# GpSimd's subtractions beside the statistics, and a written order for token groups 2 and 3, in an FNet and ReGLU kernel

## The chip, the cores and the metric

The kernel runs on one core of a Trainium2 chip. The metric is the device time of one execution in microseconds (us); lower is better. The shown time is the median of several executions.

The core's engines run side by side and wait for each other by semaphores: TensorE (PE in the profile; its weight loads are PEld), VectorE (DVE), ScalarE (ACT), GpSimd (POOL), and SyncE (SP), which issues transfers. GpSimd issues transfers too. Each engine works through its own instructions in order.

## The reference

A LayerNorm over 640 columns of 2048 tokens, and then the sum of three things: the input, the real part of a Fourier transform over columns and tokens (written as matrix products), and a gated feed-forward layer.

```python
xn = _layernorm(x, axis=-1)
# A: DFT over the hidden dim, then over the sequence, real part kept
a = jnp.einsum("bsd,ed->bse", xn, dft_hid_re)
b = jnp.einsum("bsd,ed->bse", xn, dft_hid_im)
y = jnp.einsum("ts,bse->bte", dft_seq_re, a) - jnp.einsum("ts,bse->bte", dft_seq_im, b)
# B: gated unit
gate = jnp.einsum("bsd,df->bsf", xn, W_gate); up = jnp.einsum("bsd,df->bsf", xn, W_up)
h = gate * (gate > 0) * up
return x + y + jnp.einsum("bsf,fd->bsd", h, W_down)
```

Here S = 2048 tokens, D = 640 and F = 1728; all is float32.

## The kernel before

**Three products for one.** Every float32 operand is split in two parts: a high part (a copy rounded to the matmul's format, made by ACT) and a low part (source minus high part, a subtraction, made by VectorE as a rule). A product is then three matmuls: high by high, high by low, low by high. `split` (L122) makes both parts; `mm3` (L126) issues the three matmuls at L129, L130 and L131.

**The first stage** multiplies the normalized tokens, as weights, by the DFT matrix over the sequence. The 2048 tokens are eight groups (`NG`) of two tiles of 128 tokens (`SG`). A DFT unit is one group by one chunk of 512 outputs (`CH`): a raw tile of 128 x 1024 from `in_dft`, split into a buffer of a ring of three (`cb`). A unit gives TensorE 18 matmuls: two tiles by three blocks of 128 columns by three matmuls. The stage opens with chunks 0 and 1 side by side: (chunk 0, group 0), (1, 0), (0, 1), (1, 1), (0, 2) and so on; they need one newly normalized group for each two units. Groups 0 to 3 go to the tile `xs_early`, groups 4 to 7 to `xs_late`.

**Who orders the work.** A list of steps (`todo`) is worked off by `drive(4, 2)`: in round i it emits the preparation of step i - 2, the loads of step i, and the products of step i - 4. From what is emitted a planner makes each engine's order by priority, which is the order of emission, and by the times at which it thinks operands are ready, so that a later instruction can be put ahead of one that is not ready. `pin` (`keep_in_program_order`) holds instructions in the written order; `issue_after(i)` puts what is emitted under it behind i on i's engine, without a wait.

**Normalizing a group.** `ln_stats` (L200) takes two statistics and one aggregation per tile on VectorE. `ln_root` (L206) makes the square root and two small steps on ACT, then the reciprocal and three small steps on VectorE, two of which are `scalar_tensor_tensor` on one column. Then the tokens are normalized and split into places in `xs_early` or `xs_late`. Three of five column blocks (K14) are split at once; the other two (K2) are stored unsplit by `keep_a21` (L232), a GpSimd-issued DMA, for later use.

- *Group 0* (`first_group`, L289) is written out tile by tile, since nothing else is there for TensorE to do. In each tile both chunks' low parts (L295, 128 x 512) are GpSimd's. `behind_vector` (L266) is a GpSimd marker: a multiplication of one column that VectorE's last low part wrote, so that GpSimd's subtractions behind it start only then. The second tile (L312 to L319) is scaled by ACT straight from the input for its high part and centred in place by VectorE (L222) for its low part (L317).
- *Group 1* (`second_group`, L270) is pinned too: statistics, root, ACT's high part (L280), normalization in place by VectorE (L282), the tokens' low part (L284), and last the low part of the DFT unit (0, 1) (L285).
- *Groups 2 to 7* (`layernorm`, L236) are left to the planner: VectorE normalizes one tile (L246), ACT the other (L247), ACT copies the high part (L120 called from `copy`), VectorE subtracts (L251). After group 2, ACT scales the K2 columns of group 0 into a stage tile (L258) for `keep_a21`. Group 4 to 7 load into the places of groups 0 to 3, so the load of group 4 waits for that copy.

**The products.** `first_products` (L482) and `second_products` (L455) give group 0 and unit (0, 1) to TensorE in passes: all high by high matmuls of a tile, then the next kind, so that a late low part holds up only its pass. All other units go through `product` (L465), matmul triple by matmul triple. In `first_stream` (L513) `prepare` calls these and, for chunk 1, first the layernorm of the next group, then the split of its own unit.

## Time and profile before

| | us |
|---|---|
| median of 3 runs (1050.3 to 1053.08) | 1051.42 |
| the profiled execution, its own time | 1047.28 |
| its span, first to last instruction | 1045.4 |
| TensorE busy | 1028.8 (98%) |
| VectorE busy | 802.0 (77%) |
| ACT busy | 433.2 (41%) |
| GpSimd busy | 95.5 (9%) |

The profile is of one execution. A page sums it up; views answer closer questions: a timeline of instructions (start, duration, engine, line, operation, output and inputs), a list of waits with who ended them, and the chain of work that ended last, followed back from the last instruction. Matmuls are pipelined: one of 512 columns is shown with 0.39 us, but the next starts 0.23 us later. Lines such as L124 are helpers' lines, shared by many callers.

How busy each engine is in the first 60 us, against a later stretch (us of busy time in the stretch, instructions in brackets; the last three columns are the granted TensorE clock, the DMA engines' share and GB/s):

```profile
0.00:30.00 30.00, 25.11 (x126) 19.07 (x126) 22.32 (x61) 16.66 (x33) 7.93 (x13) 1.00 0.81 304
30.00:60.00 30.00, 30.00 (x134) 24.76 (x133) 26.46 (x67) 21.55 (x38) 1.85 (x3) 1.00 0.90 342
60.00:120.00 60.00, 60.00 (x266) 49.68 (x265) 37.87 (x45) 28.55 (x38) 2.13 (x4) 1.00 0.62 195
```

The columns after the first two are PE, PEld, DVE, ACT and POOL. TensorE is idle in part of the first 30 us and in none of the next 90.

### The profile page before, as it was taken

The numbers are of one execution on the slowest core, as the hardware profiler recorded it, in microseconds if no ns is written. First come the engines' busy times: TensorE is split into PE (matmuls) and PEld (weight loads), VectorE is DVE, ScalarE is ACT, GpSimd is POOL, SyncE is SP. The second block draws the span as 40 slices with busy tenths as digits, with TensorE's granted clock in tenths as the row PEclk, the third lists the DMA queues.
The fourth block names the chain that finished last, engine by engine and source line by source line (L and its number), as shares of the span: only waits on it lengthen the run. The fifth ranks groups of instructions, "written<-read, shape, count | busy, mean of one in ns | idle before, by whom it ended". The sixth has DMA issues, their size and how long they took to land.

```text
span 1045.4 us, 12416 instructions
## 1 busy us (share of the span) xinstructions
PE 1028.8 (98%) x4528; PEld 846.1 (81%) x4528; DVE 802.0 (77%) x1073; ACT 433.2 (41%) x542; POOL 95.5 (9%) x157
## 2 busy tenths in 40 slices
PE   8999999999999999899999999999999999999998
PEld 6888888888887788688888888888888888888886
DVE  7957887978979887577887988887488667786764
ACT  5754453333333443233334544343355423552521
POOL 2100010101211001421110000100000000000000
PEclk9999999999999999899999999999999999999999
DMA  8775754957957963764355666665498636986554
GB/s 325 292 249 181 249 169 128 307 222 252 323 191 262 341 204 117 245 216 152 132 193 179 209 226 225 222 232 187 147 374 302 212 105 219 374 300 226 155 160 121
DMA packets 100157, 233.29 MB, mean 223 GB/s; under 512 B 11393, under 2 KB 50817, under 8 KB 98689
## 3 DMA queue, kind: packets, MB, share of 16 engines
q1 hardware_dynamic: 83664, 166.96, 47.9%
q0 software_dynamic: 16432, 65.55, 17.3%
q8 instruction: 35, 0.57, 0.2%
q14 instruction: 26, 0.20, 0.1%
HBM read 177.41 MB, written 54.02 MB: 221 GB/s over the span
## 4 chain that ended last, share of the span: by engine, by line
PE 87%; DVE 6%; DMA 4%; ACT 1%; issue 1%; SPq 0%; DVEq 0%; ACTq 0%
PE ps L131 29%; PE ps L130 29%; PE ps L129 28%; DMA z<-in_wgu 2%; DVE cb L124 2%; DMA tk<-in_dft 1%; PE ps L1162 1%; DVE raw L610 1%; DMA wr<-in_wd 1%; DVE tk L610 0%; ACT cb L123 0%; DVE gw L785 0%; PE ps L462 0%; DVE sa L500 0%; ACT gw L120 0%
## 5 line engine op out<-in xcount | busy, mean ns | idle before, releaser
L131 PE MATMUL ps<-cb,wt 128*128 128x512 f32 x390 | 151.9, 390 | 0.3 <-DVE wt L124 0.3
L129 PE MATMUL ps<-cb,wt 128*128 128x512 f32 x390 | 151.9, 389 | 0.0
L130 PE MATMUL ps<-cb,wt 128*128 128x512 f32 x390 | 151.7, 389 | 0.0
L124 DVE TENSOR_TENSOR cb<-rw,cb 128x1024 fp32r<-128x1024 f32 x83 | 94.0, 1133 | 68.4 <-ACT cb L123 67.8
L123 ACT ACTIVATE cb<-rw 128x1024 fp32r<-128x1024 f32 x83 | 82.0, 988 | 147.9 <-PE ps L131 124.7
L123 ACT ACTIVATE cb<-raw 128x1024 fp32r<-128x1024 f32 x77 | 81.5, 1059 | 120.3 <-PE ps L131 105.1
L124 DVE TENSOR_TENSOR cb<-raw,cb 128x1024 fp32r<-128x1024 f32 x77 | 93.8, 1220 | 42.0 <-ACT cb L123 41.7
L129 PE MATMUL ps<-xs_early,gw 128*128 128x512 f32 x260 | 101.2, 389 | 0.0
L131 PE MATMUL ps<-xs_early,gw 128*128 128x512 f32 x260 | 101.2, 389 | 0.0
L130 PE MATMUL ps<-xs_early,gw 128*128 128x512 f32 x260 | 101.1, 389 | 0.0
L130 PE MATMUL ps<-cb,xs_late 128*128 128x512 f32 x256 | 99.8, 390 | 0.9 <-DVE cb L124 0.8
L129 PE MATMUL ps<-cb,xs_late 128*128 128x512 f32 x256 | 99.6, 390 | 0.1
L131 PE MATMUL ps<-cb,xs_late 128*128 128x512 f32 x256 | 99.6, 389 | 0.0
L130 PE MATMUL ps<-cb,xs_early 128*128 128x512 f32 x238 | 92.8, 390 | 0.9 <-DVE cb L124 0.8
L129 PE MATMUL ps<-cb,xs_early 128*128 128x512 f32 x238 | 92.5, 390 | 1.2 <-ACT cb L123 1.2
L120 ACT ACTIVATE gw<-z 128x1024 fp32r<-128x1024 f32 (+1 forms) x52 | 57.8, 1111 | 84.7 <-DVE z L775 67.7
L131 PE MATMUL ps<-cb,xs_early 128*128 128x512 f32 x238 | 92.4, 389 | 0.0
L131 PEld LDWEIGHTS ps<-cb,wt 128*128 128x128 f32 x390 | 73.2, 188 | 16.0 <-DVE wt L124 0.7
L129 PEld LDWEIGHTS ps<-cb,wt 128*128 128x128 f32 x390 | 73.2, 188 | 15.4 <-ACT wt L123 0.2
L130 PEld LDWEIGHTS ps<-cb,wt 128*128 128x128 f32 x390 | 73.2, 188 | 15.2
L120 ACT ACTIVATE u<-ps 128x512 f32<-128x512 f32 x52 | 31.1, 597 | 93.4 <-PE ps L131 93.4
L785 DVE TENSOR_TENSOR gw<-z,gw 128x1024 fp32r<-128x1024 f32 (+1 forms) x52 | 64.8, 1284 | 2.2 <-ACT gw L120 2.1
(197 smaller groups left out, 1931.7 us busy)
## 6 DMA issues: line engine op xcount, KB each, us to landing
raw<-in_dft SPq DMA_DIRECT2D x94, 512.0 KB, 4.9
wt<-wparts SPq DMA_DIRECT2D x66, 256.0 KB, 3.4
z<-in_wgu SPq DMA_DIRECT2D x26, 640.0 KB, 4.0
hd<-ob POOLq DMA_DIRECT2D x26, 512.0 KB, 3.4
rw<-hd SPq DMA_DIRECT2D x24, 512.0 KB, 6.2
wparts<-pw POOLq DMA_DIRECT2D x11, 1024.0 KB, 4.1
tk<-in_dft SPq DMA_DIRECT2D x16, 512.0 KB, 6.8
rw<-pq SPq DMA_DIRECT2D x16, 512.0 KB, 7.4
```

What stands on the lines that cost most here:

```text
L120: return nc.scalar.activation(o, i, AF.Copy)
L123: nc.scalar.activation(hi, src, AF.Copy)
L124: return nc.vector.tensor_tensor(lo, src, hi.bitcast(F32), op=OP.subtract)
L129: nc.tensor.matmul(ps, wh, mh, start=first, stop=False, skip_group_check=more)
L130: nc.tensor.matmul(ps, wh, ml, start=False, stop=False, skip_group_check=more)
L131: nc.tensor.matmul(ps, wl, mh, start=False, stop=last, skip_group_check=more)
L610: sub = lambda o, i0, i1: nc.vector.tensor_tensor(o, i0, i1, op=OP.subtract)
L785: tt(self.w[:, 1, cs], self.z[:, cs], self.w[:, 0, cs].bitcast(F32), op=OP.subtract)
L1162: nc.tensor.matmul(B[key], wr[:, v, es], hr[:, cs], start=False, stop=v == 1, skip_group_check=not new)
```

## The change

Five things, all in the first stage:

1. **Group 0, first tile.** GpSimd keeps only the subtraction for chunk 0 (behind its marker). The one for chunk 1 goes to VectorE, after the second tile's root.
2. **Group 0, second tile.** VectorE no longer centres it in place: it normalizes the three K14 blocks into a stage tile (`whole`), and one subtraction makes their low part. ACT centres the two K2 blocks at the end. GpSimd still makes both chunks' low parts of this tile.
3. **Group 1.** In `next_group` VectorE makes the DFT unit's low part ahead of the normalization, no longer last.
4. **Groups 2 and 3** go through the same pinned `next_group` in place of `layernorm`: VectorE normalizes both tiles, ACT makes the high part straight from the input, and the low part of unit (0, 2) or (0, 3) is GpSimd's, in two halves behind a marker that reads the low part of unit (1, 1) or (1, 2), beside the group's statistics. The stage copy of group 0's K2 columns becomes part of group 2's pinned order.
5. **Products and order.** Units (0, 2) and (0, 3) go to TensorE in passes like (0, 1); units (1, 2) and (1, 3) are held behind those. In `prepare`, chunk 1's own split is emitted ahead of the next group's layernorm for every group, and for groups 1 to 3 behind that group's last low part. The marker writes to `root_t`.

```diff
--- before.py
+++ after.py
@@ -251,40 +251,46 @@
             low = nc.vector.tensor_tensor(xn_block(g, cs, 1), src, xn_block(g, cs, 0).bitcast(F32), op=OP.subtract)
             if g < NH:
                 keep_a21(g)
-        if g == 2:
-            with tc.issue_after(high.ins), tc.issue_after(low.ins):
-                st = stage()[:, :CH].rearrange("p (j d) -> p j d", j=SG)
-                for j in range(SG):
-                    nc.scalar.activation(st[:, j], ln_place(0)[:, j, K2], AF.Copy, scale=stat[:, 1, 0, j : j + 1])
-                keep_a21(0, st)
         if g == NG - 1:
             nc.sync.dma_start(rows.rearrange("m (g p j) -> p m g j", p=P, j=SG), stat)
 
     def pin(steps):
         return [tc.keep_in_program_order(i) for i in steps]
 
-    def behind_vector(src, o):
-
-        pin([nc.gpsimd.tensor_tensor(o, src, src, op=OP.mult)])
-
-    def second_group(b, raw):
-
-        xs, bs, mv = ln_tiles(1)
+    def behind_vector(src):
+
+        src = src.bitcast(F32)
+        pin([nc.gpsimd.tensor_tensor(root_t, src, src, op=OP.mult)])
+
+    def next_group(g, b, raw, before):
+
+        xs, bs, mv = ln_tiles(g)
         js = slice(0, SG)
-        nm, r = (stat[:, i, 1, js] for i in range(2))
+        nm, r = (stat[:, i, g, js] for i in range(2))
         nmr = mv[:, js, 6]
-        pin(ln_stats(1, xs, bs, mv, js))
+        low = lambda engine, j: pin([engine.tensor_tensor(flat(b, 1)[:, j], raw[:, j], flat(b, 0)[:, j].bitcast(F32), op=OP.subtract)])
+        pin(ln_stats(g, xs, bs, mv, js))
         pin([nc.scalar.activation(flat(b, 0), raw, AF.Copy)])
-        pin(ln_root(1, mv, js))
+        if before is not None:
+            behind_vector(before)
+            for j in range(SG):
+                low(nc.gpsimd, slice(j * CH, (j + 1) * CH))
+        pin(ln_root(g, mv, js))
         pin([nc.vector.tensor_tensor(nmr, nm, r, op=OP.mult)])
-        pin(nc.scalar.activation(xn_block(1, K14, 0)[:, j], xs[:, j, K14], AF.Identity,
-                                 bias=mv[:, j, 6:7], scale=stat[:, 1, 1, j : j + 1]) for j in range(SG))
-        pin(nc.vector.tensor_scalar(xs[:, j], xs[:, j], mv[:, j, 0:1], stat[:, 1, 1, j : j + 1],
+        pin(nc.scalar.activation(xn_block(g, K14, 0)[:, j], xs[:, j, K14], AF.Identity,
+                                 bias=mv[:, j, 6:7], scale=stat[:, 1, g, j : j + 1]) for j in range(SG))
+        if before is None:
+            low(nc.vector, slice(0, W2))
+        pin(nc.vector.tensor_scalar(xs[:, j], xs[:, j], mv[:, j, 0:1], stat[:, 1, g, j : j + 1],
                                     op0=OP.subtract, op1=OP.mult) for j in range(SG))
-        pin([nc.vector.tensor_tensor(xn_block(1, K14, 1), xs[:, :, K14], xn_block(1, K14, 0).bitcast(F32), op=OP.subtract)])
-        late["ln"] = pin([nc.vector.tensor_tensor(flat(b, 1), raw, flat(b, 0).bitcast(F32), op=OP.subtract)])[0].ins
-        late["second"] = late["ln"]
-        keep_a21(1)
+        late["ln"] = pin([nc.vector.tensor_tensor(xn_block(g, K14, 1), xs[:, :, K14], xn_block(g, K14, 0).bitcast(F32),
+                                                  op=OP.subtract)])[0].ins
+        keep_a21(g)
+        if g == 2:
+            st = stage()[:, :CH].rearrange("p (j d) -> p j d", j=SG)
+            for j in range(SG):
+                pin([nc.scalar.activation(st[:, j], ln_place(0)[:, j, K2], AF.Copy, scale=stat[:, 1, 0, j : j + 1])])
+            keep_a21(0, st)
 
     def first_group(b):
 
@@ -292,37 +298,41 @@
         xs, bs, mv = ln_tiles(0)
         part = lambda c, j: b[c][1][:, j * CH : (j + 1) * CH]
         high = lambda c, j: pin([nc.scalar.activation(b[c][0][:, 0, j], part(c, j), AF.Copy)])
-        low = lambda c, j: pin([nc.gpsimd.tensor_tensor(b[c][0][:, 1, j], part(c, j), b[c][0][:, 0, j].bitcast(F32),
-                                                        op=OP.subtract)])
-        d0, d14, rest, every = slice(0, P), slice(P, 3 * P), slice(P, D), slice(0, D)
-        for j in range(SG):
-            js = slice(j, j + 1)
-            places = [tokens(0)[:, j * XS + o : j * XS + o + D] for o in (0, D)]
-            pin(ln_stats(0, xs, bs, mv, js))
-            if j == 0:
-                pin(ln_center(0, xs, mv, 0, d0, nc.vector))
-            pin(ln_root(0, mv, js))
-            high(0, j)
-            nmr = mv[:, j, 6:7]
-            if j == 0:
-                h0, h14 = ln_scale(0, xs, j, d0), ln_scale(0, xs, j, d14)
-                pin([next(h0)])
-                pin(ln_center(0, xs, mv, 0, rest, nc.vector))
-                pin([next(h14)])
-            else:
-                pin([nc.vector.tensor_tensor(nmr, stat[:, 0, 0, js], stat[:, 1, 0, js], op=OP.mult)])
-                for cs in (d0, d14):
-                    pin([nc.scalar.activation(places[0][:, cs], xs[:, j, cs], AF.Identity, bias=nmr, scale=stat[:, 1, 0, js])])
-                pin(ln_center(0, xs, mv, j, every, nc.vector))
-                h0, h14 = (pin([nc.vector.scalar_tensor_tensor(places[1][:, cs], xs[:, j, cs], stat[:, 1, 0, js],
-                                                               places[0][:, cs].bitcast(F32), op0=OP.mult, op1=OP.subtract)])
-                           for cs in (d0, d14))
-            high(1, j)
-            pin(h0 if j == 0 else ())
-            pin(h14 if j == 0 else ())
-            behind_vector(places[1][:, 3 * P - 1 : 3 * P].bitcast(F32), mv[:, j, 6:7] if j == 0 else bs[:, 0, 0, 0:1])
-            low(0, j)
-            low(1, j)
+        low = lambda c, j, engine: pin([engine.tensor_tensor(b[c][0][:, 1, j], part(c, j), b[c][0][:, 0, j].bitcast(F32),
+                                                             op=OP.subtract)])
+        d0, d14, rest = slice(0, P), slice(P, 3 * P), slice(P, D)
+        places = lambda j: [tokens(0)[:, j * XS + o : j * XS + o + D] for o in (0, D)]
+        j0, j1 = slice(0, 1), slice(1, 2)
+        pin(ln_stats(0, xs, bs, mv, j0))
+        pin(ln_center(0, xs, mv, 0, d0, nc.vector))
+        pin(ln_root(0, mv, j0))
+        high(0, 0)
+        h0, h14 = ln_scale(0, xs, 0, d0), ln_scale(0, xs, 0, d14)
+        pin([next(h0)])
+        pin(ln_center(0, xs, mv, 0, rest, nc.vector))
+        pin([next(h14)])
+        high(1, 0)
+        pin(h0)
+        pin(h14)
+        behind_vector(places(0)[1][:, 3 * P - 1 : 3 * P])
+        low(0, 0, nc.gpsimd)
+
+        nm, r, nmr = stat[:, 0, 0, j1], stat[:, 1, 0, j1], mv[:, 1, 6:7]
+        h, l = places(1)
+        pin(ln_stats(0, xs, bs, mv, j1))
+        pin(ln_root(0, mv, j1))
+        high(0, 1)
+        pin([nc.vector.tensor_tensor(nmr, nm, r, op=OP.mult)])
+        pin(nc.scalar.activation(h[:, cs], xs[:, 1, cs], AF.Identity, bias=nmr, scale=r) for cs in (d0, d14))
+        low(1, 0, nc.vector)
+        whole = stage()[:, : 3 * P]
+        pin([nc.vector.tensor_scalar(whole, xs[:, 1, K14], mv[:, 1, 0:1], r, op0=OP.subtract, op1=OP.mult)])
+        high(1, 1)
+        pin([nc.vector.tensor_tensor(l[:, K14], whole, h[:, K14].bitcast(F32), op=OP.subtract)])
+        behind_vector(l[:, 3 * P - 1 : 3 * P])
+        low(0, 1, nc.gpsimd)
+        low(1, 1, nc.gpsimd)
+        pin(ln_center(0, xs, mv, 1, K2, nc.scalar))
 
     def token_sets(q, step, stage=stage, unit=None):
 
@@ -452,15 +462,15 @@
 
     E, F, TK, ST = {}, {}, {}, {}
 
-    def second_products(b):
+    def next_products(n, b):
 
         keys = [("e1", 0), ("e1", 1), "v1"]
         for js, vs in (((0,), (0, 2)), ((1,), (0, 2)), ((0, 1), (1,))):
             for j in js:
                 for v in vs:
                     for d, key in zip((0, 1, 4), keys):
-                        start["pe"] = pin([nc.tensor.matmul(E[0, key], xn_part(SG + j, d)[v == 1], b[:, int(v == 2), j],
-                                                            start=False, stop=False)])[0].ins
+                        start["pe"] = pin([nc.tensor.matmul(E[0, key], xn_part(n * SG + j, d)[v == 1], b[:, int(v == 2), j],
+                                                            start=False, stop=n == NH - 1 and (j, v) == (1, 1))])[0].ins
 
     def product(g, b, w, accs, first, more, extra=None):
 
@@ -540,29 +550,32 @@
                 start["b"] = [(parts(), st) for st in start["raw"]]
                 first_group(start["b"])
                 return
-            if norm == 1:
-                t1 = start[0, 1]
-                t1["b"] = parts()
-                second_group(t1["b"], t1["s"])
-            elif norm is not None:
-                layernorm(norm)
             if (n > 0 or c > 1) and "b" not in t:
                 t["b"] = b = parts()
                 with ExitStack() as order:
-                    if (c, n) == (1, 1):
-                        order.enter_context(tc.issue_after(late["second"]))
-                    split(flat(b, 0), flat(b, 1), t["s"])
+                    if c == 1 and n < NH:
+                        order.enter_context(tc.issue_after(late["ln"]))
+                    i = split(flat(b, 0), flat(b, 1), t["s"])
+                if c == 1 and n < NH - 1:
+                    late["ln"] = i.ins
+            if norm is not None:
+                if norm < NH:
+                    t1 = start[0, norm]
+                    t1["b"] = parts()
+                    next_group(norm, t1["b"], t1["s"], flat(b, 1)[:, W2 - 1 : W2] if norm > 1 else None)
+                else:
+                    layernorm(norm)
 
         def run():
             if n == 0 and c < 2:
                 first_products(c, start["b"])
                 return
-            if n == 1 and c == 0:
-                second_products(t["b"])
+            if 0 < n < NH and c == 0:
+                next_products(n, t["b"])
                 return
             accs = [(c, ("e1", i)) for i in range(2)]
             with ExitStack() as order:
-                if n == 1 and c < 2:
+                if 0 < n < NH and c == 1:
                     order.enter_context(tc.issue_after(start["pe"]))
                 product(g, t["b"], resident(n, 0), accs, half == 0, half == 1, ((c, "v1"), half, half == 0))
 
```

## The prediction

> **What bounds the kernel now.** I read the page first, then the list of waits of TensorE over the whole span, then the first 62 us instruction by instruction.

> ```profile
> span 1045.4 us, 12416 instructions
> ...
> PE 1028.8 (98%) x4528; PEld 846.1 (81%) x4528; DVE 802.0 (77%) x1073; ACT 433.2 (41%) x542; POOL 95.5 (9%) x157
> ...
> PE 87%; DVE 6%; DMA 4%; ACT 1%; issue 1%; SPq 0%; DVEq 0%; ACTq 0%
> ```

> TensorE is the bound: 98% busy and 87% of the chain that ended last. An edit ahead of it can only take away its idle time. The list of its waits says where that is:

> ```profile
> PE ps L129 <- ACT p L120: 4.2, 1, 4.2
> PE ps L462 <- DVE cb L285: 2.4, 1, 2.4
> ```

> (Columns: total, times, longest.) These are the two longest. Only the second, at the products of group 1, lies in code that the change touches. The start, in the timeline (start, duration, engine, line; the bracket is idle time and its releaser):

> ```profile
> 6.65 4.77 PE L490 MATMUL ps<-cb,xs_early 128*128 128x512 f32 x18 [0.48 <-ACT xs_early L229]
> ...
> 7.54 0.88 DVE L203 BATCH_NORM_STATS2 bs<-r 128x6 f32<-128x320 f32 x2
> ...
> 7.86 2.54 POOL L295 TENSOR_TENSOR cb<-raw,cb 128x512 fp32r<-128x512 f32 x2
> ...
> 9.30 1.12 DVE L215 SCALAR_TENSOR_TENSOR mv<-mv 128x1 f32<-128x1 f32 x1
> ...
> 10.91 0.16 DVE L313 TENSOR_TENSOR mv<-stat 128x1 f32<-128x1 f32 x1
> 11.10 0.99 ACT L315 ACTIVATE xs_early<-r,mv,stat 128x128 fp32r<-128x128 f32 x2 [1.31 <-DVE mv L313]
> ...
> 12.12 0.55 DVE L222 TENSOR_SCALAR r<-r,mv 128x640 f32<-128x640 f32 x1 [1.05 <-ACT xs_early L315]
> ...
> 12.71 0.75 DVE L317 SCALAR_TENSOR_TENSOR xs_early<-r,stat,xs_early 128x128 fp32r<-128x128 f32 x2
> ...
> 13.12 4.14 PE L490 MATMUL ps<-cb,xs_early 128*128 128x512 f32 x15 [0.24 <-DVE xs_early L317]
> 13.38 0.88 DVE L203 BATCH_NORM_STATS2 bs<-r 128x6 f32<-128x320 f32 x2
> ...
> 13.54 0.19 POOL L268 TENSOR_TENSOR bs<-xs_early 128x1 f32<-128x1 f32 x1 [3.15 <-DVE xs_early L317]
> 13.69 2.54 POOL L295 TENSOR_TENSOR cb<-raw,cb 128x512 fp32r<-128x512 f32 x2
> ...
> 16.14 0.16 DVE L215 SCALAR_TENSOR_TENSOR mv<-mv 128x2 f32<-128x2 f32 x1
> ...
> 16.80 0.16 DVE L279 TENSOR_TENSOR mv<-stat 128x2 f32<-128x2 f32 x1
> 17.00 1.30 ACT L280 ACTIVATE xs_early<-r,mv,stat 128x384 fp32r<-128x384 f32 x2 [0.89 <-DVE mv L279]
> 17.74 1.21 DVE L282 TENSOR_SCALAR r<-r,mv,stat 128x640 f32<-128x640 f32 x2 [0.78 <-ACT xs_early L280]
> ...
> 17.76 0.97 PE L462 MATMUL ps<-cb,xs_early 128*128 128x512 f32 x3 [0.50 <-ACT xs_early L280]
> ...
> 18.99 0.96 DVE L284 TENSOR_TENSOR xs_early<-r,xs_early 128x768 fp32r<-128x768 f32 x1
> 19.86 1.22 DVE L285 TENSOR_TENSOR cb<-raw,cb 128x1024 fp32r<-128x1024 f32 x1
> ...
> 21.14 3.74 PE L462 MATMUL ps<-cb,xs_early 128*128 128x512 f32 x15 [2.40 <-DVE cb L285]
> ...
> 24.71 0.39 PE L129 MATMUL ps<-cb,xs_early 128*128 128x512 f32 x1
> ```

> Two things matter. L215 on a single column takes 1.12 us beside GpSimd's subtraction, whose pair ends at 10.40, against 0.16 at 16.14: the second tile's scale L313 is late by about 1 us. And the products of group 1 wait for the DFT tile's low part (L285), the last of a chain on VectorE.

> ```profile
> 45.20 0.39 PE L129 MATMUL ps<-cb,xs_late 128*128 128x512 f32 x1
> ...
> 61.52 0.39 PE L129 MATMUL ps<-cb,xs_late 128*128 128x512 f32 x1
> ```

> Between these lie four products of 18 matmuls: 16.32 / 72 = 0.227 us each, 4.08 us a product. From 6.65 to 24.71 TensorE issues 54 of them, 12.24 us of work in 18.06: **5.8 us of idle time are all that this stage can give**, 0.55% of the time.

> **The change, part by part.**

> *Second tile of group 0.* GpSimd keeps one subtraction beside its statistics instead of two (1.27 us, half of 2.54): it ends at 9.13 and L215 starts unhindered at 9.30. It then takes 0.16, so L313 comes at 9.96 instead of 10.91 and the two ACT steps at 10.15 to 11.14. VectorE next does chunk 1's subtraction (512 wide; between the 1.22 of 1024 and the 0.96 of 768 a column costs 1.0 ns, so 0.69: ends 10.85), the 384-wide normalization into the stage (at most the 0.55 of 640; I take 0.45), and the low part (384: 0.57). It ends at 11.8; before, L317 ended at 13.46. The moved subtraction is on the path: the first tile's last three products wait for it until 10.9, where GpSimd freed them at 10.4. TensorE ends the first tile at 11.6, and all 18 of the second follow without a gap to 15.7 (before: 13.12 + 4.14 = 17.26). GpSimd's last two subtractions run 12.0 to 14.6 and are needed at 14.3 and 15.0: the first ends at 13.3, hidden. Centring of the last 256 columns goes to ACT, idle there, and nobody waits for it.

> *Group 1.* Its chain starts 1.58 us earlier (11.8 for 13.38). L279 at 15.22, ACT at 15.42, first product 0.76 behind (17.76 − 17.00) at 16.2. The DFT tile's low part now comes before the normalization, in the 0.94 us that VectorE waited for ACT (L279 to L282): 15.45 to 16.67, ahead of the 16.9 at which it is asked. So the 2.40 us wait goes. The price: normalization 16.65 instead of 16.16, low part of the tokens ready 2.21 us later (17.74 to 19.95) at 18.86; the last six products ask for it at 16.2 + 12 × 0.227 = 18.9. TensorE leaves group 1 at 16.2 + 4.1 = 20.35 instead of 24.71: **4.35 us gained here**.

> *Groups 2 and 3.* Pinned in group 1's order, with the low part of chunk 0 on GpSimd beside the statistics. From the statistics' start to the tokens' low part this chain takes 19.95 − 13.38 = 6.57 us, plus 1.2 for chunk 1's low part, so 7.77 a group on VectorE against 8.16 on TensorE. Starts: 18.86 + 1.15 = 20.0 and 27.7; the first product may start 4.38 behind (17.76 − 13.38): 24.4 and 32.1. TensorE asks at 20.35 + 4.08 = 24.43 and at 32.6; the tokens' low parts (26.6, 34.3) are asked at 27.15 and 35.3. The new wait is GpSimd's: a marker that reads the last column of chunk 1's low part (0.19, as L268 at 13.54). Behind it stand the pair and the keep-DMAs, and the products' low pass waits for the pair (22.8, asked at 25.1). Marker and pair, 2.73, fit the 16.14 − 13.38 = 2.76 to VectorE's first two-input step. So no wait, but a margin of 0.1 to 1.1 us. The new order also takes one ACT normalization per group and lets VectorE do both halves; and it moves the stage copy of group 0 and its GpSimd DMA:

> ```profile
> 28.02 0.89 ACT L258 ACTIVATE st<-r,stat 128x256 f32<-128x256 f32 x2
> ...
> 28.94 0.33 SPq L198 DMA_DIRECT2D r<-in_x  x1
> ...
> 33.66 1.28 DVE L203 BATCH_NORM_STATS2 bs<-r 128x6 f32<-128x320 f32 x3 [0.81 <-DMA r<-in_x]
> ```

> Group 4's tokens load only when this copy is done, and their statistics waited 0.81 for them. The copy now sits behind group 2's two ACT steps, at about 25 to 25.9; the load, with what queues behind it on SP, issues 3 us earlier, lands at about 30.6, and is asked at 35. On GpSimd the keep-DMAs of groups 2 and 0 fall between the pairs of 20.2 and 27.9.

> *Groups 4 to 7* keep their code, but not their place. VectorE had done group 4's statistics by the time at which it now starts them:

> ```profile
> 37.38 0.17 DVE L213 RECIPROCAL mv<-mv 128x2 f32<-128x2 f32 x1
> ...
> 38.12 0.49 DVE L203 BATCH_NORM_STATS2 bs<-r 128x6 f32<-128x320 f32 x1
> ...
> 39.65 0.60 ACT L120 ACTIVATE sa<-ps 128x512 f32<-128x512 f32 x1
> 40.15 1.27 ACT L120 ACTIVATE xs_late<-r 128x1280 fp32r<-128x1280 f32 x1
> ...
> 41.51 1.48 DVE L251 TENSOR_TENSOR xs_late<-r,xs_late 128x1280 fp32r<-128x1280 f32 x1
> ```

> Before, group 4's high part was ready at 41.42 and its low part at 42.99, and TensorE asked at 45.20: 2.2 us to spare. Now VectorE leaves group 3 at 27.7 + 7.77 = 35.4. Statistics to L213 take about 2.5 (2.76 to L215, the step behind it), L213 to the high part 41.42 − 37.38 = 4.04 before, of which 0.5 was ACT at work on another tile (40.15 − 39.65). High part ready: 35.4 + 2.5 + 3.5 = 41.4, or 42.5 if a 1.1 us subtraction falls into the chain, as one did before 37.38. TensorE asks at 32.6 + 8.16 = 40.75. **Wait 0.65 to 1.75; I take 1.15.** The low part, 1.55 later, costs nothing more if the matmuls that need it are put back, as the planner did once:

> ```profile
> 29.24 0.39 PE L129 MATMUL ps<-cb,xs_early 128*128 128x512 f32 x1
> ...
> 29.70 0.39 PE L129 MATMUL ps<-cb,xs_early 128*128 128x512 f32 x1
> ...
> 30.15 0.46 PE L131 MATMUL ps<-cb,xs_early 128*128 128x512 f32 x1
> ```

> (L131, the third product, lets L129 and L130 of the next ones pass.) From there VectorE has 7.5 us of work a group (four statistics of 0.44, small steps 1.2, one half's normalization 0.6, low part 1.48, two DFT low parts of 1.2) against 8.16, and the gain stays.

> *Sum:* −4.35 + 1.15 = −3.2 us. This profiled execution took 1047.28 (span 1045.4 and 1.9 around it), so 1044.1; it lies 4.1 below the median 1051.42 of the runs shown. From the median: 1051.42 − 3.2 = **1048.2 us**.

> [...] The row of L215 (1.12 for 0.16) shows VectorE blocked by GpSimd. [...]

> **The rivals.**

> *In time at group 4* (gain kept whole, −4.35: 1047.1). For it: VectorE had 0.81 of idle time there that goes. Against: the sums above put the high part 0.65 late at best.

> *Matmuls in order at group 4.* If the third product is not put back, TensorE waits for the low part, 42.95 to 44.1, from two matmuls in: 1.75 to 2.9 lost, gain about 2.0: 1049.4.

> *Taken back later.* Later idle time hangs on loads:

> ```profile
> 334.37 10.42 DMA tk<-in_dft
> ```

> (a piece of the chain of waits.) If such loads come at the speed of the DMA engines and not of the buffers that TensorE frees, it arrives earlier and waits longer: 1051.4. Against: loads are released by buffers that TensorE itself frees.

> *Slower: VectorE bounds groups 4 to 7.* The row at 38.12 shows the next group's statistics laid into the wait for ACT; chunk 1's low part is now emitted ahead of the layernorm. If the planner then no longer interleaves them, the chain per group is serial: 2.5 + 3.5 + 1.55 and two low parts of 1.15 = 9.85 against 8.16, 1.7 lost for each of groups 5, 6, 7 and 2.9 at group 4: 8.0 − 4.35 = 3.7 slower, 1055.1. It decides once less than 1.7 us a group of VectorE's work lies beside ACT's.

> **How the numbers follow.** Forecast 0.40, in time 0.20, in order 0.12, taken back 0.06, slower 0.22. What a measurement can tell from no change is about 0.3%, 3.15 us. The forecast's own waits (0.65 to 1.75) give gains of 3.7 to 2.6, 1047.7 to 1048.8; slightly more than half of it, 0.22, lies beyond 3.15. Faster 0.20 + 0.22 = 0.42; same 0.18 + 0.12 + 0.06 = 0.36; slower 0.22. The range reaches from 1046.0 (the in-time case and the last microsecond of the 5.8) to 1055.0, the edge of the slower case.

> **What would show it.** Right: L215 of the second tile at 0.16; no wait at group 1's products; the first of chunk 1's L129 near 20.4; TensorE idle about 1 us where it first reads xs_late, near 41 to 42. Wrong: idle time at groups 2 or 3 on GpSimd's subtraction or on ACT's steps; several waits between 41 and 70; or more idle time behind 270 us than now.

## The result, and the profile after

| | before | after |
|---|---|---|
| median (lowest to highest) of 20 executions each, us | 1052.12 (1047.22 to 1055.14) | 1051.77 (1046.84 to 1054.92) |
| profiled execution, its own time / its span, us | 1047.28 / 1045.4 | 1050.61 / 1048.8 |

The ratio of after to before is 0.9996, with a 95% interval of 0.9981 to 1.0011: no change that can be told from noise. By the ratio, after is 0.4 us faster; the interval reaches from 2.0 us faster to 1.2 us slower. The forecast was 1048.2, with a range of 1046 to 1055.

The page of after, the lines that answer to those of before:

```profile
span 1048.8 us, 12428 instructions
...
PE 1031.1 (98%) x4528; PEld 849.0 (81%) x4528; DVE 801.5 (76%) x1073; ACT 432.4 (41%) x543; POOL 99.7 (10%) x162
...
PE 84%; DVE 5%; DMA 4%; issue 3%; ACT 2%; POOL 0%; SPq 0%; DVEq 0%; ACTq 0%; POOLq 0%
```

TensorE is still the bound, with the same 4528 matmuls. The list of its waits (total, times, longest):

```profile
PE ps L129 <- ACT p L120: 4.3, 1, 4.3
PE ps L129 <- ACT xs_late L120: 2.8, 1, 2.8
...
PE ps L472 <- ACT xs_early L280: 0.3, 1, 0.3
```

The 2.4 us at the products of group 1 (L462 in before, L472 now) have become 0.3. In their place stands a new wait of 2.8 us, where TensorE first reads `xs_late`, the tokens of group 4. The start in the timeline of after (start, duration, engine, line, what; in brackets idle time and its releaser):

```profile
6.54 9.16 PE L500 MATMUL ps<-cb,xs_early 128*128 128x512 f32 x36 [0.22 <-ACT xs_early L229]
...
9.19 0.16 DVE L215 SCALAR_TENSOR_TENSOR mv<-mv 128x1 f32<-128x1 f32 x1
...
9.84 0.16 DVE L325 TENSOR_TENSOR mv<-stat 128x1 f32<-128x1 f32 x1
...
15.09 1.22 DVE L271 TENSOR_TENSOR cb<-raw,cb 128x1024 fp32r<-128x1024 f32 x1
...
15.97 4.38 PE L472 MATMUL ps<-cb,xs_early 128*128 128x512 f32 x18 [0.27 <-ACT xs_early L280]
20.18 0.39 PE L129 MATMUL ps<-cb,xs_early 128*128 128x512 f32 x1
...
24.26 4.24 PE L472 MATMUL ps<-cb,xs_early 128*128 128x512 f32 x18
...
32.42 4.24 PE L472 MATMUL ps<-cb,xs_early 128*128 128x512 f32 x18
```

The second tile's scale step L215 takes 0.16, as GpSimd's subtraction has ended (7.75 + 1.27 = 9.02, and L215 starts at 9.19). Both tiles of group 0 run as one train of 36 matmuls, and TensorE leaves group 1 at 20.18, where before left it at 24.71: 4.5 us earlier. Groups 2 and 3 show no wait (24.26 follows 18 matmuls of 0.227 behind 20.18 and 32.42 follows another 36). Then the crossing to group 4:

```profile
35.09 1.27 DVE L203 BATCH_NORM_STATS2 bs<-r 128x6 f32<-128x320 f32 x3
...
36.75 1.21 DVE L124 TENSOR_TENSOR cb<-raw,cb 128x1024 fp32r<-128x1024 f32 x1
...
37.99 1.17 DVE L124 TENSOR_TENSOR cb<-raw,cb 128x1024 fp32r<-128x1024 f32 x1
...
39.08 0.16 DVE L213 RECIPROCAL mv<-mv 128x2 f32<-128x2 f32 x1
...
40.36 0.39 PE L131 MATMUL ps<-cb,xs_early 128*128 128x512 f32 x1
40.51 0.93 ACT L247 ACTIVATE r<-r,mv,stat 128x640 f32<-128x640 f32 x1
...
41.32 1.06 ACT L123 ACTIVATE cb<-raw 128x1024 fp32r<-128x1024 f32 x1
...
42.26 1.27 ACT L120 ACTIVATE xs_late<-r 128x1280 fp32r<-128x1280 f32 x1
...
43.59 0.69 PE L129 MATMUL ps<-cb,xs_late 128*128 128x512 f32 x1 [2.84 <-ACT xs_late L120]
44.08 0.63 PE L130 MATMUL ps<-cb,xs_late 128*128 128x512 f32 x1
44.51 0.63 PE L129 MATMUL ps<-cb,xs_late 128*128 128x512 f32 x1
```

TensorE starts its last matmul of group 3 at 40.36 and could start the next at 40.59; it starts at 43.59, 3.0 us lost. Ahead of the high part (L120) lie two low parts of DFT units on VectorE (36.75 and 37.99), which put the reciprocal off to 39.08, and on ACT the copy of another DFT unit (41.32). Behind the wait the matmuls start 0.43 us apart instead of 0.23. The busy time by stretch shows why (stretch and length; PE, PEld, DVE, ACT, POOL; granted TensorE clock; DMA share; GB/s):

```profile
40.00:48.00 8.00, 5.16 (x16) 3.79 (x15) 7.78 (x21) 6.15 (x11) 1.09 (x2) 0.79 0.96 331
48.00:60.00 12.00, 12.00 (x54) 9.93 (x53) 10.19 (x23) 6.74 (x12) 0.00 (x0) 1.00 1.01 414
```

The granted clock is 0.79 in the first of these, which is half clock for 3.4 of the 8 us, and full again in the second, where TensorE has no idle time.

**Where the time goes, in one number each.** From every matmul's start to the next one's, less the 0.227 us of a matmul at full clock, is time lost, counted where the gap is at least 0.02 us too long; I added it up by stretch. Idle time and half clock are both in it. In the six profiled executions of the two kernels (four are told of further down) the time of the execution is the sum plus 1029.1 to 1029.3:

| us lost | first 60 | 330 to 365 | 430 to 450 | rest | sum | time |
|---|---|---|---|---|---|---|
| before | 5.8 | 4.3 | 6.7 | 1.3 | 18.1 | 1047.28 |
| before, again | 7.3 | 8.3 | 8.4 | 1.0 | 25.0 | 1054.31 |
| before, third | 7.2 | 4.8 | 3.8 | 1.9 | 17.8 | 1046.93 |
| after | 6.0 | 7.5 | 6.9 | 1.1 | 21.5 | 1050.61 |
| after, again | 4.4 | 7.0 | 7.4 | 0.9 | 19.8 | 1049.12 |
| after, third | 5.9 | 4.5 | 5.8 | 2.7 | 18.9 | 1048.04 |

In the first 60 us, where the change is, after loses 5.4 us on average and before 6.8. The two later stretches, whose code is unchanged, lose between 8.6 and 16.7 together in before alone; this is what spreads the executions.

### The profile page after: what moved, and what is told of

It is laid out like the page before. It is cut to its first block, busy times and chain, and to the rows that moved or that the text cites. A ratio compares the mean times of both kernels' runs of the same rounds, so it can differ in the third digit from the quotient of the medians.

```text
span 1048.8 us, 12428 instructions
## 1 busy us (share of the span) xinstructions
PE 1031.1 (98%) x4528; PEld 849.0 (81%) x4528; DVE 801.5 (76%) x1073; ACT 432.4 (41%) x543; POOL 99.7 (10%) x162
## 4 chain that ended last, share of the span: by engine, by line
PE 84%; DVE 5%; DMA 4%; issue 3%; ACT 2%; POOL 0%; SPq 0%; DVEq 0%; ACTq 0%; POOLq 0%
PE ps L130 27%; PE ps L131 27%; PE ps L129 27%; DMA z<-in_wgu 2%; DVE cb L124 1%; DMA st<-set 1%; PE ps L1175 1%; PE ps L472 1%; DMA rw<-hd 1%; ACT cb L123 1%; DMA set<-st 1%; DVE bs L203 0%; DVE raw L623 0%; DVE gw L798 0%; ACT gw L120 0%
## 5 line engine op out<-in xcount | busy, mean ns | idle before, releaser
L131 PE MATMUL ps<-cb,wt 128*128 128x512 f32 x390 | 151.9, 390 | 0.1
L129 PE MATMUL ps<-cb,wt 128*128 128x512 f32 x390 | 151.8, 389 | 0.0
L130 PE MATMUL ps<-cb,wt 128*128 128x512 f32 x390 | 151.7, 389 | 0.0
L124 DVE TENSOR_TENSOR cb<-raw,cb 128x1024 fp32r<-128x1024 f32 x75 | 91.6, 1223 | 42.2 <-ACT cb L123 41.8
L129 PE MATMUL ps<-cb,xs_late 128*128 128x512 f32 x256 | 100.6, 394 | 3.0 <-ACT xs_late L120 2.8
L130 PE MATMUL ps<-cb,xs_late 128*128 128x512 f32 x256 | 100.6, 393 | 0.9 <-DVE cb L124 0.8
L131 PE MATMUL ps<-xs_early,gw 128*128 128x512 f32 x260 | 101.2, 389 | 0.0
L130 PE MATMUL ps<-xs_early,gw 128*128 128x512 f32 x260 | 101.2, 389 | 0.0
L129 PE MATMUL ps<-xs_early,gw 128*128 128x512 f32 x260 | 101.2, 389 | 0.0
L131 PE MATMUL ps<-cb,xs_late 128*128 128x512 f32 x256 | 99.6, 390 | 0.0
L120 ACT ACTIVATE gw<-z 128x1024 fp32r<-128x1024 f32 (+1 forms) x52 | 57.8, 1111 | 84.5 <-DVE z L788 69.3
L129 PE MATMUL ps<-cb,xs_early 128*128 128x512 f32 x226 | 88.7, 394 | 1.9 <-ACT cb L123 1.9
L130 PE MATMUL ps<-cb,xs_early 128*128 128x512 f32 x226 | 88.8, 393 | 1.5 <-DVE cb L124 1.5
L131 PE MATMUL ps<-cb,xs_early 128*128 128x512 f32 x226 | 88.5, 392 | 0.0
L131 PEld LDWEIGHTS ps<-cb,wt 128*128 128x128 f32 x390 | 73.2, 188 | 15.8 <-DVE wt L124 0.5
L130 PEld LDWEIGHTS ps<-cb,wt 128*128 128x128 f32 x390 | 73.2, 188 | 15.3
L129 PEld LDWEIGHTS ps<-cb,wt 128*128 128x128 f32 x390 | 73.2, 188 | 15.1
L120 ACT ACTIVATE u<-ps 128x512 f32<-128x512 f32 x52 | 31.1, 598 | 94.3 <-PE ps L131 94.3
```

The costliest lines, as they stand in the source:

```text
L120: return nc.scalar.activation(o, i, AF.Copy)
L124: return nc.vector.tensor_tensor(lo, src, hi.bitcast(F32), op=OP.subtract)
L129: nc.tensor.matmul(ps, wh, mh, start=first, stop=False, skip_group_check=more)
L130: nc.tensor.matmul(ps, wh, ml, start=False, stop=False, skip_group_check=more)
L131: nc.tensor.matmul(ps, wl, mh, start=False, stop=last, skip_group_check=more)
```

## The experiments

Theory: the start gives 4.4 us, and TensorE, now early, pays 3.0 back waiting for group 4's high part and up to 1.5 more in the half clock behind it. Rivals: the start gain isn't real; groups 2 and 3 cost it; the time is taken back late, behind 270 us.

**One half of the change at a time.** First before with the new groups 0 and 1 only:

```diff
+        pin([nc.vector.tensor_tensor(flat(b, 1), raw, flat(b, 0).bitcast(F32), op=OP.subtract)])
         pin(nc.vector.tensor_scalar(xs[:, j], xs[:, j], mv[:, j, 0:1], stat[:, 1, 1, j : j + 1],
...
-        late["ln"] = pin([nc.vector.tensor_tensor(flat(b, 1), raw, flat(b, 0).bitcast(F32), op=OP.subtract)])[0].ins
...
+        low(0, 0, nc.gpsimd)
...
+        low(1, 0, nc.vector)
```

> Only groups 0 and 1 in the new order; groups 2 and 3, their products and the order of emission as before. Theory: the start's gain (4.4 us until group 1's products end) is whole at 20.3 us and is lost where TensorE meets fresh tokens too early. Here the planner lays group 2's and 3's statistics between other work, so the wait may come at any of groups 2 to 4; its sum is 1.5 to 4.5 us, and the ratio to before lies between 0.997 and 1.000. If it is the written order of groups 2 and 3 that costs, this kernel is clearly faster than the changed one: ratio 0.996. Rival (given back later to loads): TensorE starts chunk 2 some 4 us earlier than before and the ratio is still 1.000.

Measured: 1048.93 us, median of 12, ratio 0.9976 (0.9963 to 0.999). TensorE's timeline of this kernel:

```profile
27.35 0.51 PE L129 MATMUL ps<-cb,xs_early 128*128 128x512 f32 x1 [2.38 <-ACT xs_early L120]
27.69 0.60 PE L130 MATMUL ps<-cb,xs_early 128*128 128x512 f32 x1
28.09 0.63 PE L129 MATMUL ps<-cb,xs_early 128*128 128x512 f32 x1
28.51 0.63 PE L130 MATMUL ps<-cb,xs_early 128*128 128x512 f32 x1
```

Here the early TensorE waits one group sooner, at group 2, still in the old planned order: 2.38 us for ACT's high part, and again half clock behind it. So the old order of groups 2 and 3 can't follow the faster start, and the written order is what moves the wait on to group 4. The ratio came within the stated 0.997 to 1.000.

Then the other half, after with groups 0 and 1 as they were:

```diff
-        if before is None:
-            low(nc.vector, slice(0, W2))
...
+        if before is None:
+            late["ln"] = low(nc.vector, slice(0, W2))[0].ins
...
+            low(0, j)
+            low(1, j)
```

> Only groups 2 and 3, their products and the order of emission in the new form; groups 0 and 1 as before. Theory: the 5.7 us of idle time up to 21 us stay, TensorE reaches group 4 near 45 us, and its high part (near 43 us) is there in time: no wait, no half clock, time as before, ratio 1.000 (0.999 to 1.001). Rival (the written order of groups 2 and 3 costs by itself): a wait of 1 us or more at group 4 here too, ratio 1.002 or more.

Measured: 1052.89 us, median of 12, ratio 1.0017 (1.0001 to 1.0032): not a gain, by itself a small loss, larger than the theory allowed (0.999 to 1.001) and just short of the rival's 1.002. Its trace has no wait at group 4, which was the rival's sign. Its wait at group 1's products is that of before, and the products behind it ran at half clock in this execution (6.41 us for what took 3.74 in before):

```profile
21.07 6.41 PE L468 MATMUL ps<-cb,xs_early 128*128 128x512 f32 x15 [2.42 <-DVE cb L271]
```

The two halves point the same way. With the written order of groups 2 and 3, 0.9976 becomes 0.9996, and 1.000 becomes 1.0017: about 2 us more each time, at the edge of what these intervals can tell. This is not lost in the first 60 us, where the profiled executions of the first half and of after both lose 6.0. So the rival that this order costs something by itself is not ruled out, and by which mechanism it would is not shown.

**Group 4 first.** If the wait at group 4 takes the gain, it must come back when the DFT units' splits are put behind group 4's own steps. After, with the low part of unit (0, 4) behind the root step of group 4 and the splits of (1, 4) and (0, 5) behind its high and low part:

```diff
+            if g == NH:
+                late["four"] = high.ins, low.ins
...
+                    if (c, n) == (0, NH):
+                        order.enter_context(tc.issue_after(late["ln"]))
+                    if (c, n) in ((1, NH), (0, NH + 1)):
+                        for after in late["four"]:
+                            order.enter_context(tc.issue_after(after))
```

> The changed kernel, but the DFT low parts and copies of units (0,4), (1,4) and (0,5) are put behind the steps of group 4 that they had been laid into. Theory: VectorE's chain is shorter by two subtractions of 1.15 us and ACT's by one copy of 0.95, so TensorE's wait at group 4 falls from 2.84 to 1 us or less, the half clock behind it does not come (1.7 us), chunk 2 starts 3.5 us earlier than in the changed kernel, and the ratio to before is 0.996 to 0.9975. Rival (given back later): chunk 2 starts earlier, idle time behind 270 us grows by as much, ratio 0.9995 to 1.0005.

Measured: 1047.75 us, median of 5, ratio 0.9963 (0.995 to 0.9976).

```profile
42.35 0.50 PE L129 MATMUL ps<-cb,xs_late 128*128 128x512 f32 x1 [1.48 <-ACT xs_late L120]
42.69 0.40 PE L130 MATMUL ps<-cb,xs_late 128*128 128x512 f32 x1
```

The wait fell to 1.48, not to 1 or less: one subtraction (38.40 to 39.62) still lies between group 4's last small step and its normalization. The matmuls behind it are at full clock. The first 288 of the large matmuls, the two opening chunks, are done at 75.5 us, 2.5 us earlier than in the profiled after (78.0), not 3.5. A second version puts that subtraction behind the normalization too:

```diff
-            nc.vector.tensor_scalar(xs[:, 0], xs[:, 0], mv[:, 0, 0:1], stat[:, 1, g, 0:1], op0=OP.subtract, op1=OP.mult)
+            scaled = nc.vector.tensor_scalar(xs[:, 0], xs[:, 0], mv[:, 0, 0:1], stat[:, 1, g, 0:1], op0=OP.subtract, op1=OP.mult)
...
+                    if (c, n) == (0, NH):
+                        order.enter_context(tc.issue_after(late["scaled"]))
```

> As the kernel with group 4's chain ahead, but unit (0,4)'s subtraction stands behind group 4's normalization and no longer between its root and its normalization. Theory: ACT's half starts 1.15 us earlier, TensorE's first matmul on xs_late comes at 41.2 (was 42.35, and 43.59 in the changed kernel), the wait is 0.5 us or less, and 1 us more is gained: ratio to before 0.995 to 0.996. Rival (VectorE is full, so the wait only moves): a wait of 1 us or more at group 5 or 6, ratio as before, 0.9963.

```profile
41.58 0.50 PE L129 MATMUL ps<-cb,xs_late 128*128 128x512 f32 x1 [0.70 <-ACT xs_late L120]
```

Measured: 1046.77 us, median of 8, ratio 0.9949 (0.9931 to 0.9967), 5.4 us faster than before by the ratio, and the best version found. The wait is 0.70, a little more than expected. Its profiled execution loses 2.5 us in the first 60, where before lost 5.8 to 7.3. The wait that was left in after was a matter of the order at group 4. How much of the 5.4 us comes from that order, and how much from half clock that no longer follows a wait, the next experiment bears on.

**The wait kept, TensorE kept busy.** To tell the half clock from the wait, after with 44 small matmuls on the tile of zeros `warm` between unit (1, 3) and unit (0, 4). Their results are not used.

```diff
+                if (c, n) == (0, NH):
+                    order.enter_context(tc.issue_after(start["fill"]))
...
+            if (c, n) == (1, NH - 1):
+                with tc.issue_after(last.ins):
+                    ps = bank()
+                    for i in range(FILL):
+                        start["fill"] = nc.tensor.matmul(ps[:, :P], warm, warm, start=True, stop=True).ins
```

> The changed kernel with 44 small bf16 matmuls on zeros (128 columns, into a free bank) behind unit (1,3), in the wait for group 4. Theory: the wait for group 4 stays (first matmul on xs_late near 43.6 us), but TensorE is not idle in it, so the matmuls behind it come each 0.23 us and not each 0.43: 1.7 us less, ratio to before near 0.998. If the slow matmuls have another cause than the idle time, they stay slow and the ratio is as the changed kernel's, 0.9996.

```profile
40.72 2.63 PE L589 MATMUL ps<-warm 128*128 128x128 bf16 x44
43.72 0.50 PE L130 MATMUL ps<-cb,xs_late 128*128 128x512 f32 x1 [0.37 <-ACT xs_late L121]
44.06 0.40 PE L131 MATMUL ps<-cb,xs_late 128*128 128x512 f32 x1
```

Group 4 is reached no earlier, at 43.72 (43.59 in after), the matmuls behind it are at full clock, and the median is 1047.28 of 6, ratio 0.9959 (0.9945 to 0.9973), lower than the 0.998 of the theory. The same for before, 36 of them in its wait at group 1's products:

```diff
+                    if (j, v) == (0, 0):
+                        ps = bank()
+                        pin(nc.tensor.matmul(ps[:, :P], warm, warm, start=True, stop=True) for i in range(FILL))
```

> The kernel before, with 36 small bf16 matmuls on zeros in TensorE's wait of 2.4 us at group 1's products (behind the first three of them). Nothing else is moved. Theory: part of what lifts the median of the kernel before over its profiled execution is the half clock that this wait brings in some executions (seen in the run with only groups 2 and 3 changed: 15 matmuls in 6.41 us in place of 3.74). Then this kernel's runs lie closer together and its median 2 to 3 us lower, ratio 0.997 to 0.998, granted clock 0.996 in most runs. Rival (the wait alone counts, the clock is chance of single runs): ratio 0.9995 to 1.0015, spread as before.

```profile
18.53 2.18 PE L467 MATMUL ps<-warm 128*128 128x128 bf16 x36
```

Measured: 1047.24 us, median of 7, ratio 0.9961 (0.9943 to 0.9978), lower than I had expected. Two things follow. With the waits filled the two kernels are level, 1047.28 and 1047.24. And filling one wait is worth some 4 us (0.39% of 1051.8), though the half clock that follows directly accounts for some 1.5 where it lasts 3.4 us: seven matmuls at 0.427 instead of 0.227, 1.4 us, in after. The granted clocks of all executions tell where part of the other 2.5 lies: their mean is 0.9938 over the 14 executions of before in that batch and 0.9961 over the 7 with the wait filled. Over 1050 us that is 2.4 us, an estimate from these two means. So the filling saves half clock elsewhere in the execution too; the rest stays open.

This also limits what the version with group 4 first shows. It is at 0.9949 (0.9931 to 0.9967), and before with nothing but its wait filled at 0.9961 (0.9943 to 0.9978): the totals can't tell the two apart.

**The price of GpSimd's subtraction.** After, with the subtraction for chunk 1 of the first tile back on GpSimd:

```diff
         low(0, 0, nc.gpsimd)
+        low(1, 0, nc.gpsimd)
...
-        low(1, 0, nc.vector)
```

> The changed kernel with the first tile's subtraction for chunk 1 back on GpSimd, behind the one for chunk 0. Theory (VectorE's first two-input step stands still while GpSimd subtracts): L215 of the second tile takes 1.1 us and not 0.16, the second tile's scale comes 0.9 to 1.0 us later, the subtraction of 0.69 leaves VectorE, so the second tile's low part comes some 0.3 us later and group 1's products end within 0.5 us of the changed kernel's (20.1 us). Rival (the move to VectorE is what gained the start): group 1's products end 1 us later or more.

```profile
9.31 1.12 DVE L215 SCALAR_TENSOR_TENSOR mv<-mv 128x1 f32<-128x1 f32 x1
...
10.93 0.16 DVE L326 TENSOR_TENSOR mv<-stat 128x1 f32<-128x1 f32 x1
...
12.15 0.56 DVE L331 TENSOR_TENSOR xs_early<-st,xs_early 128x384 fp32r<-128x384 f32 x1 [0.67 <-ACT xs_early L327]
...
17.02 4.15 PE L472 MATMUL ps<-cb,xs_early 128*128 128x512 f32 x17 [0.47 <-ACT xs_early L280]
```

L215 is at 1.12 again and ends with GpSimd's pair (9.31 + 1.12 = 10.43 and 7.87 + 2.54 = 10.41), its scale step (L326 here) at 10.93 for 9.84, and group 1's products start at 17.02 for 15.97: 1.05 us later, and they end at 21.23 (20.18). This execution began 0.12 us later (first product at 6.66 for 6.54), so the edit costs about 0.9, near the rival's 1 us and not within the 0.5 of my theory. I had counted the 0.7 of the moved subtraction as saved on VectorE; it is not, since VectorE then waits 0.67 for ACT at L331 instead. One time: 1052.7.

**GpSimd's pairs in groups 2 and 3.** After, with the low parts of units (0, 2) and (0, 3) on VectorE:

```diff
-                    next_group(norm, t1["b"], t1["s"], flat(b, 1)[:, W2 - 1 : W2] if norm > 1 else None)
+                    next_group(norm, t1["b"], t1["s"], None)
```

> The changed kernel with the low parts of units (0,2) and (0,3) back on VectorE, in the order of group 1 (ahead of the normalization), so GpSimd subtracts nothing in groups 2 and 3. Theory: VectorE had to wait 0.78 us for ACT at that place in each of the two groups, so each subtraction of 1.22 costs it only 0.44; group 4's statistics start 0.9 us later, and TensorE's first matmul on xs_late comes at 44.5 (43.59 in the changed kernel). Rival (GpSimd's pairs are worth their full 1.22 each): 46.0.

```profile
44.02 0.50 PE L129 MATMUL ps<-cb,xs_late 128*128 128x512 f32 x1 [3.20 <-ACT xs_late L120]
44.36 0.40 PE L130 MATMUL ps<-cb,xs_late 128*128 128x512 f32 x1
```

The pairs bring the crossing forward by 0.3 to 0.4 us (from 44.02 to 43.59, 43.67 and 43.69 in the three profiles of after), not by the 0.9 of my theory, nor by the 2.4 of the two subtractions (1.22 each) that they take from VectorE. One time: 1050.46. No half clock is seen here behind the longest wait of all, 3.20.

**Each kernel twice more, unchanged.** Single profiles had to stand for a spread of 8 us so far.

> The kernel before, unchanged, profiled once more. My theory: its wait of about 2.4 us at the products of group 1 brings TensorE's half clock in many executions, and the execution profiled first was one of those without. Then at least two of the four executions profiled in this batch (two of each kernel) show half clock (matmuls 0.43 us apart, for 3.4 or 6.8 us) right behind their unfilled wait of the first 50 us, and an execution with it takes 1 to 3 us more than one without (before: about 1047.3 without, 1049 to 1051 with). Rival: the half clock there has nothing to do with that wait, and comes in none or one of the four.

> The kernel before once more. The same as for the run ahead of it: with half clock behind the wait at group 1's products 1049 to 1051, without it near 1047.3; the later idle time at 330 to 365 us, 3.8 to 8.1 us so far, adds its own spread.

> The changed kernel, unchanged, profiled once more. My theory: a wait of 2.6 to 3.2 us where TensorE first reads xs_late (its place and length are set by ACT's order and do not vary by more than 0.4 us), and half clock behind it in some executions only. Rival: the wait itself varies by more than 1 us between executions, so that the single profile told too little of it.

> The changed kernel once more: a wait of 2.6 to 3.2 us where TensorE first reads xs_late, as for the run ahead of it; where half clock at about 354 us is there, 1.5 us more in that stretch than where it is not.

TensorE's timeline of before, the second profile and then the third:

```profile
21.07 5.30 PE L462 MATMUL ps<-cb,xs_early 128*128 128x512 f32 x15 [2.42 <-DVE cb L285]
26.20 0.40 PE L129 MATMUL ps<-cb,xs_early 128*128 128x512 f32 x1
```

```profile
21.13 5.20 PE L462 MATMUL ps<-cb,xs_early 128*128 128x512 f32 x15 [2.41 <-DVE cb L285]
26.18 0.39 PE L129 MATMUL ps<-cb,xs_early 128*128 128x512 f32 x1
```

And of after, the second and then the third:

```profile
43.69 0.50 PE L129 MATMUL ps<-cb,xs_late 128*128 128x512 f32 x1 [2.85 <-ACT xs_late L120]
44.03 0.40 PE L130 MATMUL ps<-cb,xs_late 128*128 128x512 f32 x1
```

```profile
43.67 0.79 PE L129 MATMUL ps<-cb,xs_late 128*128 128x512 f32 x1 [2.84 <-ACT xs_late L120]
44.27 0.63 PE L130 MATMUL ps<-cb,xs_late 128*128 128x512 f32 x1
44.69 0.63 PE L129 MATMUL ps<-cb,xs_late 128*128 128x512 f32 x1
```

The waits hardly vary: 2.40, 2.42 and 2.41 in before, 2.84, 2.85 and 2.84 in after; the rival that the single profile misled about the wait falls. The half clock comes and goes: 2 of 3 in before, 2 of 3 in after. The execution of before on which the prediction was built is the one without it, and so left group 1 at 24.71, where the other two left it at 26.2. The half clock cost 1.5 us at either place. But my expectation that it alone sets the time, 1049 to 1051 with it, missed both ways: 1054.31 and 1046.93. The later stretches of the table weigh more. There, executions with half clock near 354 us lose 7.0 to 8.3 us at 330 to 365 and those without it 4.3 to 4.8, so the 1.5 us that I had expected between them was too little as well.

## Why the prediction came out as it did

**Right: the start.** L215 took 0.16, as said; L325 came at 9.84 (9.96 forecast), group 1's scale step L279 at 15.01 (15.22), its first product at 15.97 (16.2), and chunk 1's first L129 at 20.18 (20.35). The DFT unit's low part does fit into VectorE's wait for ACT (L271 at 15.09). The experiment with both subtractions on GpSimd shows that the 1.1 us of that step are worth about 0.9 at the products. The rows show that L215 takes 1.12 beside GpSimd's pair and 0.16 where the subtraction has ended; why it does is not shown.

**Right: groups 2 and 3.** No wait on GpSimd or on ACT, as the x18 trains at full clock show, and group 4's statistics start at 35.09 (35.4) without waiting for their load. The pairs of GpSimd did not hold VectorE up either: they end at 22.25 and 29.95, and L215 takes 0.17 at 22.16 and 0.16 at 30.23.

**Wrong: the wait at group 4.** The step that failed is "Wait 0.65 to 1.75; I take 1.15". TensorE asked when it was said to, 40.6 (40.75), but the high part was ready at 43.53 (42.26 + 1.27), not at 41.4 to 42.5. Two terms were short. The reciprocal came at the upper end of what I had allowed, 39.08 for 37.9 to 39.0, since VectorE laid not one but two DFT subtractions, 2.4 us, among the steps ahead of it. And from there to the high part it took 4.45 us (39.08 to 43.53), not 3.5, which put it a full 1.0 beyond that end: I had taken off 0.5 of ACT's work on another tile that before showed, and in its place came ACT's copy of a DFT unit, 1.06. So 3.0 us were lost instead of 1.15. The versions with group 4 first, which take those pieces away, show both: the wait goes from 2.84 to 1.48 and 0.70. Their medians, 1047.75 and 1046.77 for 1051.77, fall by more than that. Part of the rest is granted clock: its mean over their executions is 0.9960 and 0.9955, over those of after 0.9937.

With this one term put right the sum is −4.35 + 3.0 = −1.35 us, or 1050.1 from the median shown, and 0.9987 as a ratio, inside the measured 0.9981 to 1.0011. The first 60 us of the three profiles each say nearly the same: 6.8 lost before, 5.4 after, with half clock behind the wait in two of three on both sides. The measured time lies in the range of 1046 to 1055 because that range was wide; the forecast gain of 3.2 us lies outside the measured interval.

**Not priced: half clock.** I read the wait of 2.40 at group 1's products as 2.40 us, and the new one at its length. In two of three profiles each costs 1.5 more. As this falls on both kernels it hardly moves their difference. It does show that one profile is a poor base for a figure of 1 us: the first 60 us lost 5.8 in that execution and 7.2 to 7.3 in the other two.

**The rivals.** *In time at group 4* falls, by 3.0 us. *Matmuls in order* falls: L131 is put back (44.08, 44.51), as forecast. *VectorE bounds groups 4 to 7* falls: TensorE has no idle time in 48 to 60. *Taken back later* is not needed to explain the total, but it is not excluded. The first version with group 4 first loses only 3.4 us in the first 60 and then 14.4 in the two later stretches together, against 8.6 to 16.7 in before; the second version loses 2.5 and 11.6. The later idle time varies by 8 us between executions of the same kernel, so that three profiles of each can't exclude a part of 1 us.

**Open.** Near 354 us a half clock of 3.4 us is seen in 6 of the 10 profiles that have an unfilled wait of 2.38 us or more in the first 50 us, and in none of the 4 whose wait was shortened or filled. In each of the six, TensorE has idle time of its own there, just ahead of the half clock (the last section has the numbers). Why there is more of it in these six is not known; nothing here was tried on it. What the written order of groups 2 and 3 costs is open too.

## What to carry to other kernels

A stage that is made faster reaches the next stage's operands sooner: work out when those are ready with everything that the planner may lay ahead of them, above all pieces that their own engines do for other units, and put the first of them first. Here this took the wait from 2.84 to 0.70 us. Where a wait can't be removed, keeping TensorE busy in it may be worth more than the wait's length suggests: in either kernel that alone gave about 4 us, so that most of the 5.4 us of the best version can't be credited to the order. And before a figure of a few us is built on one profile, take two or three more of the same kernel and see which of its waits and clocks repeat.

## What the runs showed of the hardware

Half clock came behind waits of TensorE of 2.38 to 2.85 us. Those waits were followed by matmuls 0.43 us apart, for 3.4 us and once for 6.8 (only groups 2 and 3 changed: a granted clock of 0.72 from 15 to 27 us), in 7 of the 9 profiles with such a wait unfilled (before 2 of 3, after 2 of 3, the two halves of the change, and the one with GpSimd's second subtraction); in the one at 3.20 the matmuls came 0.23 us apart. At waits of 0.70 and 1.48, and at waits filled with small matmuls, no half clock followed (matmuls 0.23 us apart behind the 1.48; a granted clock of 1.00 from 40 to 48 us with the 0.70 and with after's filled wait, and from 15 to 27 with before's). So the length of the wait alone does not decide it.

So what counts in these traces is how much of one period is idle, with the border near 2.0 of 3.4 us. In after, 3.0 us of idle time fell into one period, and half clock followed. In after, again, an edge divided the same wait into periods with 2.0 and 1.1, and none followed. The wait of 3.20 was divided too, 1.6 and 1.9. Near 354 us the period ahead of each of the six half clocks holds 2.04 to 2.79, and in the other eight profiles no period there holds more than 2.05. No experiment moved a wait against the periods.
